# Attention and mixture of experts on one core: the second product's order of blocks, and the place of one copy on ScalarE

## The chip, the cores and the metric

The kernel runs on one core of a Trainium2 chip. The metric is the device time of one execution in microseconds (us). A core has five engines with a queue each: TensorE (PE, with PEld for its weight loads), VectorE (DVE), ScalarE (ACT), GpSimd (POOL) and SyncE (SP, which issues most of the DMAs). Each queue is worked off in its order, and an engine waits for another by a semaphore. TensorE multiplies into PSUM; ScalarE and VectorE read PSUM, GpSimd works in SBUF alone.

## The reference

```
attention, for each of 8 batches and 8 heads (S = 576, head size 64):
    scores = q k^T / 8 + cum[i] - cum[j]        # cum: cumulative sum of log(clip(f))
    out    = softmax(causal(scores)) v
x = all heads of a position side by side        # N = 4608 rows, D = 512
logits = x @ w_gate;  expert = argmax(logits);  gate = its softmax value
for e in range(8):                              # w1: 512 x 1024, w2: 1024 x 512
    xe = x[expert == e]
    out[expert == e] = gate * (relu(xe @ w1[e]) @ w2[e])
```

## The kernel before

Attention over all batches takes the first 340 us of the span, and expert 0 is worked in between and to 366 us. From there on experts 1 to 7 follow one another, each some 55 us long, and 6.6 us of closing work end the span. The change lies in experts 1 to 7 alone.

An expert has room for 640 rows. All matrices are kept as a rounded high part and the rest as a low part, so that one product takes three matmuls: high with high, high with low, low with high.

**First product** (`sevens`, `group`, `product`; its matmuls are L1421). x @ w1 is done with seven products of half-size blocks in the place of eight. The 1024 columns of h are eight blocks of 128, and group i (0 to 3) makes the blocks i and i + 4. A group has seven steps (s = 0 to 6) of six matmuls with 256 to 320 columns. They write four banks of PSUM, called a, b, g and d here: steps 0 to 3 start a, b, g, d, and steps 4 to 6 add to a, b, g. PE's order is steps 0 to 3 of group 0, then steps 4 to 6 of a group with steps 0 to 3 of the next in one branch, and last steps 4 to 6 of group 3.

What the other engines do is in `after(s)`, and is written into the queues in the order of the steps:

- s = 0: what is left of the group before (the list `self.ends`), and `p1 <- a` by ScalarE (L1475), the copy of the first product. Step 4 adds to a, so PE has to wait for this copy.
- s = 1: u2 = b + p1 by VectorE (L1479), which step 5 waits for; then `last` of the group before.
- s = 2: `p5 <- g` by ScalarE (L1482), which step 6 waits for. p1 and p5 are two buffers that all groups share.
- s = 4: ScalarE rectifies a into the high part of h (L1466), VectorE makes the low part, called the rest (L1469).
- s = 5: u3 = b + p1 (L1488) and d = u3 - d (L1489) by VectorE, p5 = u3 + p5 by GpSimd (L1490).
- s = 6: the rectifications left over go into `self.ends`: `end` (ScalarE rectifies d and p5; VectorE does g = g + u2, L1498, and the rest of d), then the rectification of g, then `last` (the rests of p5 and g). They run at s = 0 and 1 of the next group, and those of group 3 at the start of the second product.

The two halves of block i come from a and g, those of block i + 4 from d and p5. Between these steps ScalarE rounds weights (L1333, L1348), VectorE or GpSimd makes their low parts (L1339, L1349), GpSimd forms sums of the next expert's first weights (L1318 to L1321) and fetches its rows.

**Second product** (`down`; its matmuls are L1229). Five tiles of 128 rows; each runs over the eight blocks of h, three matmuls of 512 columns a block, into one bank, which ScalarE scales (L1237) and GpSimd scatters (L1238). In quarters of two blocks, work for the next expert is put in between: after the quarters 0, 2, 4, 6 and 8 PE turns 128 rows of it by four transposes (L1390) into one of the two banks of the pool `ps_t`, from which ScalarE and VectorE make the operands of its first product (`turn_t`, the last operation on the bank is the L1398 that writes xa).

The order on each engine is the order of the program's lines, with the lists `ups` (by step of the first product) and `dns` (by quarter of the second) setting what comes between.

Of the kernel before, what the change touches and what calls it, by code (L numbers as in the profile page):

```python
# [37 lines left out]
FT = FF // P  # L38
# [135 lines left out]
def psum(pool):  # L174
    return pool.tile([P, 512], F32, name="ps", tag="ps")
# [893 lines left out]
class Moe:  # L1069
# [149 lines left out]
    def down(self, e, m, part=(0, FT)):  # L1219

        c, nc = self.c, self.nc
        rows = self.rows_of_h(e, m)
        if part[0] == 0:
            self.py[m] = psum((c.ps_v, c.ps_m)[m % 2])
        py = self.py[m]
        for ft in range(*part):
            w = self.w2p[e, ft]
            for k, (hi_, wi) in enumerate(((0, 0), (0, 1), (1, 0))):
                c.note(nc.tensor.matmul(  # L1229
                    py, rows(hi_, ft), w[wi],  # L1230
                    start=(ft + k == 0), stop=(ft == FT - 1 and k == 2),
                ))
        if part[1] < FT:
            return
        _, si, g, s = self.index(e, m)
        y = c.yp.tile([P, D], F32, name="y")
        nc.scalar.activation(y, py, AF.Copy, scale=g[:, s : s + 1])  # L1237
        nc.gpsimd.indirect_dma_start(  # L1238
            out=self.out, out_offset=bass.IndirectOffsetOnAxis(ap=si[:, s : s + 1], axis=0),
            in_=y, in_offset=None, bounds_check=self.x_dram.shape[0] - 1, oob_is_err=False,  # L1240
        )
# [26 lines left out]
    def finish(self, run, t):  # L1268

        c = self.c  # L1270
        ends = []
        fx, lg = t["fx"], t["lg"]

        def indices():
            self.idx["all"] = table_indices(c, self.tc, c.rp, c.tab, NHI, "fast")
            arms(c, self.tc)
            self.begin_x(0, 1)
            for e, m in ((0, NA), (0, NA + 1), (1, 3), (1, 4)):
                self.fetch(e, m)

        up = lambda ft: lambda: self.up(0, 0, ft)
        down = lambda m, *part: lambda: self.down(0, m, part)
        turn = lambda m: lambda: ends.append(self.turn(0, m))
        end = lambda: ends.pop(0)()
        for f in (
            t["logits"], up(2), lambda: self.load_w2(0, 3),
            lg, t["softmax"], t["expert"], up(3), fx[0], t["gate"], up(4), t["rank"], fx[1],
            t["slot"], up(5), t["hi"], fx[2], t["lo"], up(6), fx[3], lambda: self.split_w2(0, 3),
            up(7), t["table"], fx[4], down(0, 0, 4), indices, down(0, 4, 8), down(1, 0, 4),
            down(1, 4, 8), down(2, 0, 4),  # L1290
            turn(NA), end, down(2, 4, 5), turn(NA + 1), end, down(2, 5, 8),
        ):
            run(f)
# [152 lines left out]
    def group(self, e, i):  # L1446

        c, nc = self.c, self.nc
        V, A, G = nc.vector, nc.scalar, nc.gpsimd
        pools = (c.ps_t, c.ps_t, c.ps_m, c.ps_v) if i % 2 == 0 else (c.ps_s,) * 3  # L1450
        a, b, g, d = [psum(p) for p in pools] + [c.ps_r] * (i % 2)
        a, b, g, d = (t[:, 0:HN] for t in (a, b, g, d))

        late = (e, i) == (1, 0)
        p1, p5 = (
            c.yp.tile([P, D], F32, name="y")[:, 0:HN] if late and k == 1 else c.values["u", k]
            for k in range(2)
        )
        us = {}
        hh, hl = self.h[e]  # L1460

        def place(h, f, n):
            return h[:, f * (FT // 2) + i].rearrange("p (s j) -> p j s", j=2)[:, n]

        def relu(src, *at):
            A.activation(place(hh, *at), src, AF.Relu)  # L1466

        def rest(src, *at):
            V.scalar_tensor_tensor(place(hl, *at), src, 0.0, place(hh, *at).bitcast(F32),  # L1469
                                   ALU.max, ALU.subtract)  # L1470

        def after(s):
            if s == 0:
                self.ends.pop(0)()
                A.copy(p1, a)  # L1475
                self.ends.pop(0)()
            elif s == 1:
                us[2] = self.up_.tile([P, HN], F32, name="u2")
                V.tensor_tensor(us[2], b, p1, ALU.add)  # L1479
                self.ends.pop(0)()  # L1480
            elif s == 2:
                A.copy(p5, g)  # L1482
            elif s == 4:
                relu(a, 0, 0)
                rest(a, 0, 0)
            elif s == 5:
                u3 = self.up_.tile([P, HN], F32, name="u3")
                V.tensor_tensor(u3, b, p1, ALU.add)  # L1488
                V.tensor_tensor(d, u3, d, ALU.subtract)  # L1489
                G.tensor_tensor(p5, u3, p5, ALU.add)  # L1490
            elif s == 6:
                self.ends = [end, lambda: relu(g, 0, 1), last]

        def end():
            relu(d, 1, 0)
            if not late:
                relu(p5, 1, 1)
            V.tensor_tensor(g, g, us[2], ALU.add)  # L1498
            rest(d, 1, 0)

        def last():
            if late:
                relu(p5, 1, 1)
            rest(p5, 1, 1)
            rest(g, 0, 1)

        steps = ((a, 0, 0, "B11", True), (b, 0, 1, "T2", True), (g, 0, 2, "T1", True),
                 (d, 0, 3, "T4", True), (a, 1, 0, "B21", False), (b, 1, 1, "T3", False),
                 (g, 1, 2, "B22", False))
        return steps, after  # L1510
# [333 lines left out]
```

## Time and profile before

| what | us |
|---|---|
| median of 3 runs | 757.97 (757.63 to 758.67) |
| profiled execution | 760.25 |
| its span, first to last instruction | 758.5 |
| PE busy | 739.9 (98%) |
| DVE, ACT, POOL busy | 542.4 (72%), 499.2 (66%), 514.8 (68%) |
| mean granted clock | 0.991 |
| expert 1, 366.2 to 424.5 | 58.3, PE busy 56.35, clock 0.97 |
| expert 2, 424.5 to 479.6 | 55.1, PE busy 54.68, clock 1.00 |
| expert 3, 479.6 to 534.2 | 54.6, PE busy 52.98 |
| expert 5, 589.3 to 643.7 | 54.4, PE busy 51.49 |

A matmul's record overlaps the next one's, since matmuls are pipelined: in a full stretch 512 columns are done every 0.23 us, though one record lasts 0.40. The distance between two starts tells the pace, and a pause shows as a longer distance.

### The profile page before, as it was taken

The page shows a single profiled execution, that of the slowest core. Times are in us where ns is not written, and L with a number is a line of the kernel's source. Part 1 is how long each engine was busy: PE and PEld are TensorE (multiplying, and loading weights), DVE is VectorE, ACT ScalarE, POOL GpSimd, SP SyncE. Part 2 cuts the span into 40 slices and gives each one's busy share as a digit, 9 for nine tenths or more (in the row PEclk, how much of TensorE's full clock was granted, in tenths as well). Part 3 has the DMA queues.
Part 4 walks back from the last instruction along what each step waited for, and adds up shares of the span by engine and source line. Part 5 has one row for each costly group of instructions (what it writes and reads, how often), then busy time and mean ns, then how long its engine had stood idle before and what let it go on. Part 6 is the DMA issues. An engine that isn't in the chain of part 4 may idle for free.

```text
span 758.5 us, 18648 instructions
## 1 busy us (share of the span) xinstructions
PE 739.9 (98%) x6464; PEld 632.8 (83%) x6464; DVE 542.4 (72%) x1596; ACT 499.2 (66%) x1319; POOL 514.8 (68%) x681
## 2 busy tenths in 40 slices
PE   8999999999999999999989999999999989999996
PEld 4888888888888888889988998978988978988975
DVE  6668898988898887625897488487586685784720
ACT  6999998989898987434665465455554653654621
POOL 6999998989898979644784574475465565565311
PEclk9999999999999999999999999999999999999998
DMA  6857778767766676243343523623622623523200
GB/s 199 215 150 206 198 206 198 211 197 199 209 201 208 194 204 182 96 136 103 123 161 111 176 76 112 195 71 97 202 83 89 209 81 104 168 85 106 73 29 34
DMA packets 78563, 111.85 MB, mean 147 GB/s; under 512 B 9327, under 2 KB 40047, under 8 KB 78448
## 3 DMA queue, kind: packets, MB, share of 16 engines
q1 hardware_dynamic: 71408, 90.38, 41.3%
q0 software_dynamic: 6400, 19.93, 8.0%
q8 instruction: 71, 1.16, 0.7%
q14 instruction: 44, 0.36, 0.1%
q10 hardware_dynamic: 640, 0.01, 0.0%
HBM read 91.26 MB, written 20.07 MB: 147 GB/s over the span
## 4 chain that ended last, share of the span: by engine, by line
PE 72%; DVE 15%; POOL 6%; ACT 3%; issue 2%; DMA 0%; POOLq 0%; DVEq 0%; ACTq 0%
PE ps L1229 27%; PE ps L525 11%; PE ps L402 9%; PE ps L454 7%; PE ps L1421 5%; DVE w_1w L1349 5%; PE ps L436 4%; DVE hl L1469 4%; POOL u L1490 3%; PE ps L449 2%; PE ps L1195 2%; ACT hhw L1466 2%; DVE w1s L1339 2%; POOL w L1086 1%; DVE u L1488 1%
## 5 line engine op out<-in xcount | busy, mean ns | idle before, releaser
L421 ACT ACTIVATE sc<-sc,nmx 128x512 f32<-128x512 f32 (+3 forms) x256 | 142.6, 560 | 5.2 <-DVE nmx L378 4.0
L1238 POOL DMA_INDIRECT out<-y,si_fast x40 | 42.0, 1050 | 119.4 <-ACT y L1237 74.9
L1229 PE MATMUL ps<-w_0w,hhw 128*128 128x512 f32 x280 | 114.2, 408 | 5.9 <-ACT hhw L1466 5.9
L1229 PE MATMUL ps<-w_0w,hl 128*128 128x512 f32 x280 | 111.3, 398 | 0.0
L1229 PE MATMUL ps<-w_1w,hhw 128*128 128x512 f32 x280 | 111.1, 397 | 0.0
L1421 PE MATMUL ps<-X_0w,w1s 128*128 128x320 f32 (+2 forms) x504 | 107.4, 303 | 0.2 <-ACT u L1482 0.2
L466 ACT COPY aT<-ps 128x512 f32<-128x512 f32 (+1 forms) x224 | 93.3, 506 | 1.9 <-PE ps L454 1.2
L329 POOL TENSOR_TENSOR hl<-raw,hl 128x640 fp32r<-128x640 f32 (+1 forms) x60 | 89.6, 1493 | 5.0
L525 PE MATMUL ps<-aT,va_t 128*64 128x256 f32 (+3 forms) x896 | 90.3, 353 | 0.0
L1421 PEld LDWEIGHTS ps<-X_0w,w1s 128*128 128x128 f32 x504 | 82.2, 188 | 0.8 <-ACT u L1482 0.4
L1237 ACT ACTIVATE y<-ps,g_fast 128x512 f32<-128x512 f32 x40 | 27.6, 691 | 81.8 <-PE ps L1229 76.2
L402 PE MATMUL ps<-hl 64*128 64x512 f32 (+1 forms) x720 | 80.1, 340 | 0.0
L525 PEld LDWEIGHTS ps<-aT,va_t 128*64 128x64 f32 x896 | 56.1, 137 | 28.5 <-issue 5.0
L1421 PE MATMUL ps<-X_1w,w1s 128*128 128x320 f32 (+2 forms) x252 | 75.8, 301 | 0.0
L1229 PEld LDWEIGHTS ps<-w_0w,hhw 128*128 128x128 f32 x280 | 52.8, 188 | 19.2 <-ACT hhw L1466 9.0
L378 DVE CUSTOM_DVE_ANT_0 sc<-ps,bias 128x128 f32<-128x128 f32 (+1 forms) x128 | 59.8, 486 | 9.2 <-PE ps L402 2.4
L1229 PEld LDWEIGHTS ps<-w_0w,hl 128*128 128x128 f32 x280 | 53.0, 189 | 14.4 <-DVE hl L1469 2.1
L1490 POOL TENSOR_TENSOR u<-u,u 128x320 f32<-128x320 f32 x27 | 23.8, 881 | 59.0 <-DVE u L1488 55.5
L1229 PEld LDWEIGHTS ps<-w_1w,hhw 128*128 128x128 f32 x280 | 53.0, 189 | 10.2
L378 DVE CUSTOM_DVE_ANT_1 sc<-ps,bias 128x256 f32<-128x256 f32 (+1 forms) x128 | 57.7, 487 | 2.8 <-PE ps L402 2.8
L1421 PE MATMUL ps<-xa,w1s 128*128 128x320 f32 (+2 forms) x336 | 56.2, 302 | 3.0 <-ACT u L1475 3.0
L1339 DVE TENSOR_TENSOR w1s<-w1r,w1s 128x1024 fp32r<-128x1024 f32 (+1 forms) x42 | 49.1, 1183 | 11.9 <-ACT w1s L1333 10.2
(247 smaller groups left out, 1894.0 us busy)
## 6 DMA issues: line engine op xcount, KB each, us to landing
bias<-ud SPq DMA_DIRECT2D x30, 576.0 KB, 7.0
w1r<-in_w SPq DMA_DIRECT2D x112, 128.0 KB, 2.9
w<-in_w SPq DMA_DIRECT2D x28, 512.0 KB, 4.2
raw<-in_qkT SPq DMA_DIRECT2D x64, 160.0 KB, 3.2
raw<-in_qkT SPq DMA_DIRECT2D x64, 144.0 KB, 3.7
va_t<-in_va SPq DMA_DIRECT2D x32, 256.0 KB, 5.8
x_dram<-row SPq DMA_DIRECT2D x32, 256.0 KB, 2.8
wraw<-in_w SPq DMA_DIRECT2D x7, 512.0 KB
```

The costliest lines, as they stand in the source:

```text
L329: return eng.tensor_tensor(hl[:, 1], raws[n][:, r : r + w], hl[:, 0].bitcast(F32), ALU.subtract)
L378: red_last[:] = [V.tensor_tensor_reduce(dst, src, in1, -0.125, init, ALU.add, ALU.min, nms[n][:, col : col + 1]).ins]
L402: note(nc.tensor.matmul(pb[j][:, o : o + w], q[js], k[js], start=(i == 0), stop=(i == len(terms) - 1),))
L421: A.activation(x, x, AF.Exp, bias=nms[n][:, 5 * j + t : 5 * j + t + 1], scale=-1.0, accum_out=ssums[b][:, t, 2 * p + j : 2 * p + j + 1])
L454: note(nc.tensor.transpose(out.bitcast(F32R), words, c.identr[rows, rows]))
L466: copy_on = {"a": lambda o, i: A.copy(o, i), "v": lambda o, i: V.tensor_copy(o, i)}
L525: note(nc.tensor.matmul(pv[j * HD : (j + 1) * HD, q0 - qa : qb - qa], l, r, start=(blk == 0), stop=(blk == nb - 1),))
L1229: c.note(nc.tensor.matmul(py, rows(hi_, ft), w[wi], start=(ft + k == 0), stop=(ft == FT - 1 and k == 2),))
L1238: nc.gpsimd.indirect_dma_start(out=self.out, out_offset=bass.IndirectOffsetOnAxis(ap=si[:, s : s + 1], axis=0), in_=y, in_offset=None, bou ...
L1339: (eng or self.nc.vector).tensor_tensor(lo, raw, hi.bitcast(F32), ALU.subtract)
L1421: self.nc.tensor.matmul(bank[:, 0:cols], w[:, wi, mat, kt], x[xi][:, kt, 0:cols], start=start and k == 0, stop=k == 5, skip_group_check=True,)
L1490: G.tensor_tensor(p5, u3, p5, ALU.add)
```

## The change

In experts 1 to 7 each tile of the second product takes the blocks in the order 0, 1, 2, 4, 5, 6, 3, 7, so that the two blocks of group 3 come last; expert 0 keeps its order. And at s = 0 ScalarE copies p1 ahead of `end` of the group before, where it stood between `end` and the rectification of g.

```
         if part[0] == 0:
             self.py[m] = psum((c.ps_v, c.ps_m)[m % 2])
         py = self.py[m]
-        for ft in range(*part):
+        for n in range(*part):
+            ft = (0, 1, 2, 4, 5, 6, 3, 7)[n] if e else n
             w = self.w2p[e, ft]
             for k, (hi_, wi) in enumerate(((0, 0), (0, 1), (1, 0))):
                 c.note(nc.tensor.matmul(
                     py, rows(hi_, ft), w[wi],
-                    start=(ft + k == 0), stop=(ft == FT - 1 and k == 2),
+                    start=(n + k == 0), stop=(n == FT - 1 and k == 2),
                 ))
...
         def after(s):
             if s == 0:
+                A.copy(p1, a)
                 self.ends.pop(0)()
-                A.copy(p1, a)
                 self.ends.pop(0)()
```

All lines below the first piece stand one line further down in the changed kernel, up to the copy.

PE in the first tile of an expert's second product, after its first two blocks; w_0 are the weights of blocks 0 to 3, w_1 those of 4 to 7, hhw and hl the high and the low part of h. Before:

```order
L1390 MATMUL ps<-identr,xg 128x128 [waits DMASW1_49,PE_49]
L1390 MATMUL ps<-identr,xg 128x128 x3
L1229 MATMUL ps<-w_0_0w,hhw 128x512
L1229 MATMUL ps<-w_0_1w,hhw 128x512
L1229 MATMUL ps<-w_0_0w,hl 128x512 [waits DVE_49]
L1229 MATMUL ps<-w_0_0w,hhw 128x512 [waits Activation_49]
L1229 MATMUL ps<-w_0_1w,hhw 128x512
L1229 MATMUL ps<-w_0_0w,hl 128x512 [waits DVE_49]
L1229 MATMUL ps<-w_1_0w,hhw 128x512
```

Now:

```order
L1391 MATMUL ps<-identr,xg 128x128 [waits DMASW1_49,PE_49]
L1391 MATMUL ps<-identr,xg 128x128 x3
L1230 MATMUL ps<-w_0_0w,hhw 128x512
L1230 MATMUL ps<-w_0_1w,hhw 128x512
L1230 MATMUL ps<-w_0_0w,hl 128x512 [waits DVE_49]
L1230 MATMUL ps<-w_1_0w,hhw 128x512
...
L1391 MATMUL ps<-identr,xg 128x128 [waits DMASW2_49,PE_49]
L1391 MATMUL ps<-identr,xg 128x128 x3
L1230 MATMUL ps<-w_0_0w,hhw 128x512 [waits Activation_49]
L1230 MATMUL ps<-w_0_1w,hhw 128x512
L1230 MATMUL ps<-w_0_0w,hl 128x512 [waits DVE_49]
```

Block 3, whose first matmul waits for ScalarE and its third for VectorE, moved from behind block 2 to behind the second set of transposes.

ScalarE at the last change of group in an expert's first product, from the rectification of a; pr is d, u_104 is p5, u_96 is p1, ps the banks a and g. Before:

```order
L1466 ACTIVATE hhw<-ps 128x320 [waits PE_49]
L1466 ACTIVATE hhw<-ps 128x320 [waits DVE_49]
L1466 ACTIVATE hhw<-u_104 128x320 [waits Pool_49]
L1475 COPY u_96<-ps 128x320 [waits PE_49]
L1466 ACTIVATE hhw<-ps 128x320 [waits DVE_49]
L1348 CAST w_1_0w<-w_1_1_102 128x1024 [waits DMAHW6_49]
L1482 COPY u_104<-ps 128x320 [waits DVE_49,PE_49,Activation_49]
```

Now:

```order
L1467 ACTIVATE hhw<-ps 128x320 [waits PE_49]
L1475 COPY u_96<-ps 128x320 [waits DVE_49,PE_49]
L1467 ACTIVATE hhw<-ps 128x320 [waits DVE_49]
L1467 ACTIVATE hhw<-u_104 128x320 [waits Pool_49]
L1467 ACTIVATE hhw<-ps 128x320 [waits DVE_49]
L1349 CAST w_1_0w<-w_1_1_102 128x1024 [waits DMAHW6_49]
L1483 COPY u_104<-ps 128x320 [waits DVE_49,PE_49]
```

The copy of p1 moved ahead of the rectifications of d and p5, and waits for VectorE now, which reads p1 last in u3 of the group before. The order on VectorE and GpSimd is the same as before.

## Rows read from the trace of the kernel before

**Rows 1.** Waits of the whole span: waiter, what it waited for, total us, times, longest
```profile
PE ps L1229 <- ACT hhw L1466: 5.9, 7, 1.7
PE ps L1421 <- ACT u L1475: 3.0, 5, 1.0
```

**Rows 2.** Timeline, PE, expert 3: start, length, line, operation, [idle before <-releaser]
```profile
503.22 0.40 PE L1229 MATMUL ps<-w_0w,hhw 128*128 128x512 f32 x1
...
505.45 0.40 PE L1229 MATMUL ps<-w_0w,hl 128*128 128x512 f32 x1
506.88 0.50 PE L1229 MATMUL ps<-w_0w,hhw 128*128 128x512 f32 x1 [1.03 <-ACT hhw L1466]
...
507.82 0.39 PE L1229 MATMUL ps<-w_0w,hhw 128*128 128x512 f32 x1
```

**Rows 3.** Timeline, PE, first tile of expert 1's second product
```profile
393.72 0.40 PE L1229 MATMUL ps<-w_0w,hl 128*128 128x512 f32 x1
395.83 0.64 PE L1229 MATMUL ps<-w_0w,hhw 128*128 128x512 f32 x1 [1.72 <-ACT hhw L1466]
...
399.58 0.46 PE L1390 MATMUL ps<-identr,xg 128*128 128x128 f32 x4
```

**Rows 4.** Windows: stretch, length, busy PE, PEld, DVE, ACT, POOL, clock, DMA, GB/s
```profile
397.00:398.20 1.20, 1.20 (x4) 0.91 (x4) 0.96 (x4) 1.20 (x3) 1.04 (x3) 0.50 0.00 0
```

**Rows 5.** Timeline, PE, block 3 of expert 7's first tile
```profile
725.49 0.50 PE L1229 MATMUL ps<-w_0w,hhw 128*128 128x512 f32 x1 [0.47 <-ACT hhw L1466]
```

**Rows 6.** Timeline, ScalarE and VectorE, expert 3: the last rectifications and rests
```profile
506.01 0.49 ACT L1466 ACTIVATE hhw<-u 128x320 fp32r<-128x320 f32 x1 [0.83 <-POOL u L1490]
506.40 0.43 ACT L1466 ACTIVATE hhw<-ps 128x320 fp32r<-128x320 f32 x1
...
506.94 0.48 DVE L1469 SCALAR_TENSOR_TENSOR hl<-ps,hhw 128x320 fp32r<-128x320 f32 x1
```

**Rows 7.** Timeline, PE, expert 3: last matmul of step 3, step 4, step 6
```profile
499.82 0.29 PE L1421 MATMUL pr<-X_1w,w1s 128*128 128x288 f32 x1
500.70 1.06 PE L1421 MATMUL ps<-xa,w1s 128*128 128x288 f32 x6 [0.59 <-ACT u L1475]
...
502.40 0.44 PE L1421 MATMUL ps<-X_0w,w1s 128*128 128x288 f32 x2
```

**Rows 8.** Timeline, VectorE, then ScalarE, same change of group
```profile
498.28 0.48 DVE L1488 TENSOR_TENSOR u<-ps,u 128x320 f32<-128x320 f32 x1
...
500.68 0.49 DVE L1479 TENSOR_TENSOR u<-ps,u 128x320 f32<-128x320 f32 x1 [0.37 <-ACT u L1475]
...
499.32 0.46 ACT L1466 ACTIVATE hhw<-ps 128x320 fp32r<-128x320 f32 x1 [2.26 <-DVE ps L1489]
...
500.25 0.40 ACT L1475 COPY u<-ps 128x320 f32<-128x320 f32 x1
...
501.83 0.44 ACT L1482 COPY u<-ps 128x320 f32<-128x320 f32 x1
```

**Rows 9.** Timeline, GpSimd and VectorE, same place: sum of weights, rest of p5
```profile
500.58 0.74 POOL L1319 TENSOR_TENSOR w1r<-w1r 128x256 f32<-128x256 f32 x1
501.09 0.58 DVE L1469 SCALAR_TENSOR_TENSOR hl<-u,hhw 128x320 fp32r<-128x320 f32 x1
```

**Rows 10.** Timeline: fifth transposes (PE), last readers of turns 1 and 3 (DVE), experts 3, 1
```profile
518.67 0.46 PE L1390 MATMUL ps<-identr,xg 128*128 128x128 f32 x4
...
508.99 0.42 DVE L1398 TENSOR_TENSOR xa<-ps,xa 128x256 fp32r<-128x256 f32 x1
...
516.56 0.42 DVE L1398 TENSOR_TENSOR xa<-ps,xa 128x256 fp32r<-128x256 f32 x1
...
409.04 0.46 PE L1390 MATMUL ps<-identr,xg 128*128 128x128 f32 x4
...
397.93 0.42 DVE L1398 TENSOR_TENSOR xa<-ps,xa 128x256 fp32r<-128x256 f32 x1
...
405.98 0.42 DVE L1398 TENSOR_TENSOR xa<-ps,xa 128x256 fp32r<-128x256 f32 x1
```

More of the change, by code (lines that the diff above doesn't have):

```diff
@@ L1225, in down @@
         py = self.py[m]
-        for ft in range(*part):
+        for n in range(*part):
+            ft = (0, 1, 2, 4, 5, 6, 3, 7)[n] if e else n
             w = self.w2p[e, ft]
@@ L1230, in down @@
                     py, rows(hi_, ft), w[wi],
-                    start=(ft + k == 0), stop=(ft == FT - 1 and k == 2),
+                    start=(n + k == 0), stop=(n == FT - 1 and k == 2),
                 ))
@@ L1473, in after @@
             if s == 0:
+                A.copy(p1, a)
                 self.ends.pop(0)()
-                A.copy(p1, a)
                 self.ends.pop(0)()
```

## The prediction

> **What bounds the kernel now.** I read in this order: the mean granted clock (0.991, and nearly all of the span at full clock), the share of busy time (PE 98%), the waits of PE, then PE's rows in order of time at each wait, then ScalarE, VectorE and GpSimd at the same places. PE is the bound nearly everywhere, so its stalls are lost time, and only two kinds fall in experts 1 to 7: seven waits of the second product for a rectification (L1466), and five of the first product for the copy of L1475 [rows 1]. The view counts only what is left after the modelled end of the matmul before, 5.9 and 3.0 us. The loss is larger, from start to start.
>
> In expert 3 the second product starts at 503.22. Its first nine matmuls and one set of transposes take 2.46 us (505.45 and one step of 0.23 more). Block 3 should follow at 505.68, starts at 506.88, and its last part waits for VectorE; block 4 starts at 507.82 instead of 506.38 [rows 2]. The loss is **1.44 us**. Done in the same way, experts 2, 4, 5, 6 and 7 lose 0.84, 0.84, 1.55, 1.12 and 0.89 us (the last of the seven is shown [rows 5]). In expert 1 the gap of 2.1 us is followed by nine matmuls at 0.43 us a step [rows 3], at a granted clock of 0.50, that is 1.2 GHz [rows 4]. From 393.72 to the transposes at 399.58 there are 5.86 us for ten steps, which are 2.30 at full clock: a loss of **3.56 us**, of which about 1.65 is the slow clock. All seven: **10.24 us**.
>
> What ends this wait last is a chain outside PE: GpSimd's sum (L1490) lets ScalarE rectify p5 at 506.01, behind it g at 506.40 (block 3's second half, done at 506.83), and VectorE's rest of g is done at 507.42 [rows 6].
>
> **The change, part by part.** *Order of the blocks.* No instruction is added. Block 3 becomes the seventh of eight. Two runs of nine matmuls and a transpose set stand ahead of it then, 4.9 us after the product's start (in expert 7, which turns no rows, 18 steps or 4.2). In expert 3 that is 508.1; the rectification is done at 506.83, the rest 0.6 later and is read two steps after the first matmul [rows 2, 6]. Slack 1.3 us: the stall goes. Expert 1 is the tightest: its chain ends 4.3 us after the start, and I find the slack to be about nothing there, which costs at most some 0.3 us. With no gap of two microseconds, I expect the slow clock to go too. Blocks 4 to 6 are read earlier by one place; they and their weights were written microseconds before. In the last tile block 3 is read 2.1 us later, so the loads of the next expert's second weights, which overwrite it, wait longer; they are first rounded nine steps of the first product later (some 8 us), and a load of this size lands in 4.2 us. This costs nothing.
>
> *The copy ahead of the rectifications.* In expert 3's last change of group VectorE finishes u3 (L1488) at 498.76, the last thing that the copy's destination waits for, and ScalarE waits for VectorE's L1489 until 499.32. The copy of 0.40 us fits into that idle time, from 498.80, instead of at 500.25 [rows 8]. So the step-4 wait goes (0.75 us from 499.82 to 500.70, less one step of 0.13, and 0.1 for the slow restart after it [rows 7]). But the wait does not vanish, it moves. Step 6 needs the copy of p5 (L1482), which was done at 502.27 [rows 8]; PE without the first wait would want it at 501.54, 0.86 before the 502.40 at which step 6 started [rows 7]. ScalarE could do that copy 0.3 us earlier, since everything behind L1475 moves up by its 0.30. It also overwrites what VectorE's rest of p5 still reads, and that ends at 501.67.
>
> Will this rest come earlier, now that VectorE's L1479 no longer waits 0.37 for the copy [rows 8]? The trace says no: it took 0.58, against 0.48 of the same operation with an input in PSUM [rows 6], and ended 0.35 after GpSimd's L1319, which ended at 501.32 [rows 9]. GpSimd's place hangs on L1490, which the change doesn't move. The Trainium skill, "SBUF — State Buffer", section "SBUF: two separate sides", states it as a lock: a VectorE operation with two SBUF inputs and a GpSimd operation that reads SBUF exclude one another for a whole instruction. By that rule, the trace agrees, the 0.37 us is swallowed; without it the chain would run 0.3 us ahead, and the sum below would be 0.9 us larger.
>
> So the copy of p5 runs at 501.71 to 502.15 and step 6 at 502.19: a gain of 0.21 us, not 0.85. In the same way I get 0.36, 0.12 and 0.40 us for experts 1, 5 and 7; experts 2, 4 and 6 have no such wait. Bounds of this part: the whole of it, about 4.4 us start to start, if nothing took its place; and a loss, because at an expert's first change of group PE is not ahead: there the rectifications now stand behind a copy that waits for PE's step 0, and come some 0.3 us later. The same lock swallows that too; if not, the chain is 0.3 us late and three experts lose 0.3 each. I take the nearer end, the rows above.
>
> *What is late next.* The chain of ScalarE, VectorE and GpSimd does not get faster, PE does. After the stall the five transposes of the second product share two banks of PSUM, and the fifth needs the third's, which VectorE frees with the last operation of that turn. In expert 3 it ends at 516.98 and the fifth transposes stood at 518.67 [rows 10]. PE may gain 518.67 − 517.02 = **1.65 us** there, just what the two terms (1.44 + 0.21) ask for. Expert 5 has the same 1.65. In expert 1 the third turn would be freed at 406.44, and 0.48 earlier where it no longer waits for PE (from the first turn to the third it takes 8.05 us there and 7.57 in expert 3): 405.96, against 409.04, so of 3.56 + 0.36 only **3.08 us** can be had [rows 10]. Experts 2, 4, 6 have 0.5 to 0.8 us to spare.
>
> *Sum:* 3.08 + 0.84 + 1.65 + 0.84 + 1.65 + 1.12 + (0.89 + 0.40) = **10.5 us**. The profiled execution took 760.25 us, 1.75 more than its span; it would take 749.8. The runs' median is 757.97, 2.3 below the profiled one; taking the same from it gives **747.5 us**.
>
> **The rivals.** *The chain does not hold PE back.* Then all stalls and the copy's gains stand: 10.24 + 1.09 = 11.3 us, 746.6; and if p5's copy did not hold PE either, 743.4. For: a bank's last reader is inferred from the code and the order. Against: the rows of the chain show hardly any slack in expert 1.
>
> *The chain comes later.* Each us costs one us in experts 1, 3 and 5, whose transposes then wait. Half a microsecond gives 749.0; the slow clock staying in expert 1 costs 0.8 more, 749.8. For: the late rectifications at an expert's first change. Against: in these places VectorE waits for GpSimd anyway [rows 9].
>
> *Slower than before.* The mechanism is the copy heading ScalarE's queue: where PE's step 0 of the next group is late, both rectifications and VectorE's rests wait behind it. A chain late by d loses 7d − 3.0 of the 10.5 us (all seven experts past their slack), so it decides at d = 1.9 us in an expert; at 2.3 the time is 760.6. Three changes of group would have to lose over 0.6 each. Against: only the first finds PE behind, by 0.3; at the last, VectorE's u3 (498.76) comes well after PE has done step 0 of the next group, since PE only waits two steps of work later [rows 7].
>
> That the change does not do what it says is no rival: the order of instructions shows both moves in all seven experts.
>
> **How the numbers follow.** About 0.2% (1.5 us) can be told from no change. Forecast, 747.5 with its own range of 746.5 to 748.7: 0.6. The chain not binding, 743.4 to 746.6: 0.15. The chain later or the clock still low, 748.7 to 752: 0.22. Slower: 0.03. The range takes the forecast, most of the second and most of the third, 744.8 to 750.8. Faster 0.95, same 0.03, slower 0.02 (part of the slower rival ends within 0.2%).
>
> **What would show it.** Right: no wait of PE's L1229 for L1466 left, or one of under 0.4 us in expert 1; full granted clock after expert 1's second product starts; waits for L1475 replaced by shorter ones for L1482 in experts 1, 3, 5 and 7; short waits of the transposes for VectorE's L1398 in expert 1. Wrong: block 3 still waits by over 0.5 us, waits for L1482 that are as long as those for L1475 were, the transposes of experts 2, 4 or 6 waiting, or new waits of the first product for weights or for turned rows.

## The result, and the profile after

Three comparisons, each beside the kernel before:

| changed kernel, median us | before, median us | difference | ratio, 95% interval |
|---|---|---|---|
| 750.67 (4 runs) | 758.32 (4 runs) | 7.65 | 0.9895 [0.9877, 0.9912] |
| 749.19 (4 runs) | 759.44 (17 runs) | 10.25 | 0.9861 [0.9844, 0.9879] |
| 749.99 (5 runs) | 758.40 (9 runs) | 8.41 | 0.9890 [0.9873, 0.9908] |

The 13 runs of the changed kernel have a median of 749.99 us, the 30 of the kernel before in these comparisons one of 758.82: 8.83 us less. The forecast of 747.5 us was 2.5 too low. The time lies inside the stated range of 744.8 to 750.8, by the first comparison (750.67) only just, and the sign was right.

The waits of PE after (columns as in [rows 1]; lines behind the first piece of the diff are one higher now):

```profile
PE ps L1422 <- ACT u L1483: 1.9, 4, 0.8
...
PE ps L1422 <- DVE u L1480: 0.3, 1, 0.3
PE ps L1391 <- ACT X_0w L1401: 0.2, 1, 0.2
PE ps L1391 <- issue: 0.2, 1, 0.2
```

Both rows of [rows 1] are gone: the second product (now L1230) has no wait for a rectification left, and none of the first product is for the copy of p1. New are four waits for the copy of p5 (L1483), one of 0.3 us for VectorE's u2 (L1480), and two small ones of transposes (L1391), one after the other in expert 1.

Windows after: expert 1, expert 3, and the stretch of expert 1 in which the gap of [rows 3] stood (columns as in [rows 4]):

```profile
366.80:421.98 55.18, 54.78 (x310) 48.60 (x309) 43.26 (x79) 30.52 (x61) 38.77 (x39) 1.00 0.41 133
476.30:529.70 53.40, 52.98 (x310) 46.80 (x309) 38.58 (x76) 29.49 (x60) 31.79 (x32) 1.00 0.40 129
391.60:396.80 5.20, 5.20 (x29) 4.27 (x28) 4.98 (x10) 1.93 (x6) 4.87 (x5) 1.00 0.19 52
```

Expert 1 went from 58.1 to 55.2 us, expert 3 from 54.5 to 53.4. PE is busy through the third window, at full clock, where 2.1 us lay between two starts before.

PE after in expert 1: the second product's start, the second transposes and block 3 behind them (its first matmul and its third, which reads the rest), the last two transposes; then what block 3 needs from ScalarE and VectorE, and VectorE's last reads of the banks of turns 2 and 3:

```profile
391.67 0.39 PE L1230 MATMUL ps<-w_0w,hhw 128*128 128x512 f32 x1
...
396.21 0.45 PE L1391 MATMUL ps<-identr,xg 128*128 128x128 f32 x4
396.50 0.47 PE L1230 MATMUL ps<-w_0w,hhw 128*128 128x512 f32 x1
...
397.03 0.39 PE L1230 MATMUL ps<-w_0w,hl 128*128 128x512 f32 x1
...
402.85 0.51 PE L1391 MATMUL ps<-identr,xg 128*128 128x128 f32 x4 [0.18 <-issue]
...
406.44 0.51 PE L1391 MATMUL ps<-identr,xg 128*128 128x128 f32 x4 [0.20 <-ACT X_0w L1401]
```

```profile
395.75 0.44 ACT L1467 ACTIVATE hhw<-ps 128x320 fp32r<-128x320 f32 x1
...
396.30 0.48 DVE L1470 SCALAR_TENSOR_TENSOR hl<-ps,hhw 128x320 fp32r<-128x320 f32 x1
...
402.33 0.42 DVE L1399 TENSOR_TENSOR xa<-ps,xa 128x256 fp32r<-128x256 f32 x1
...
405.92 0.42 DVE L1399 TENSOR_TENSOR xa<-ps,xa 128x256 fp32r<-128x256 f32 x1
```

Block 3 starts 4.83 us after the product does. The last rectification was done at 396.19, so it had 0.3 us to spare, and the last rest (done at 396.78) is read at 397.03. What is late next are the last two transposes: the steps between the five are 3.17, 3.15, **3.49** and **3.59** us, where 3.15 is the undisturbed one. The profile names ScalarE's L1401 for one of these two waits and nothing for the other. But VectorE's L1399, the last reader of the bank that each of them needs, ends at 402.75 and 406.34, 0.10 us ahead of the transposes both times; the forecast had named it (L1398 before).

The last change of group in expert 3 after, on PE, ScalarE, VectorE, GpSimd:

```profile
498.28 0.29 PE L1422 MATMUL ps<-X_1w,w1s 128*128 128x288 f32 x1
499.00 0.53 PE L1422 MATMUL ps<-X_0w,w1s 128*128 128x288 f32 x2 [0.42 <-ACT u L1483]
...
495.60 0.43 ACT L1475 COPY u<-ps 128x320 f32<-128x320 f32 x1 [1.79 <-DVE u L1489]
...
497.32 1.04 ACT L1349 CAST w_0w<-w 128x1024 fp32r<-128x1024 f32 x1
498.52 0.43 ACT L1483 COPY u<-ps 128x320 f32<-128x320 f32 x1 [0.17 <-DVE hl L1470]
...
497.37 1.06 DVE L1470 SCALAR_TENSOR_TENSOR hl<-u,hhw 128x320 fp32r<-128x320 f32 x1
...
497.34 0.74 POOL L1320 TENSOR_TENSOR w1r<-w1r 128x256 f32<-128x256 f32 x1
```

The copy of p1 stands in ScalarE's idle time, as forecast. The copy of p5 waits for VectorE's rest of p5, which ends at 498.43, and that is 0.35 us after GpSimd's sum, as in [rows 9]. Measured from the start of expert 3's first product (476.32 here, 479.63 before), the copy of p5 starts at 22.20 us in both kernels.

Expert 7 turns nothing for a next expert, and GpSimd forms no sums there. VectorE and ScalarE after, the same place in expert 7:

```profile
712.20 0.48 DVE L1470 SCALAR_TENSOR_TENSOR hl<-u,hhw 128x320 fp32r<-128x320 f32 x1
...
712.14 1.04 ACT L1349 CAST w_0w<-w 128x1024 fp32r<-128x1024 f32 x1
713.07 0.43 ACT L1483 COPY u<-ps 128x320 f32<-128x320 f32 x1
```

The same rest takes 0.48 us in place of 1.06, and the copy of p5 is held by ScalarE's rounding instead.

### The profile page after: what moved, and what is told of

Its sections match the earlier page's. It is cut to its first block, busy times and chain, and to the rows that moved or that the text cites. A ratio compares the mean times of both kernels' runs of the same rounds, so it can differ in the third digit from the quotient of the medians.

```text
span 749.4 us, 18668 instructions
## 1 busy us (share of the span) xinstructions
PE 736.5 (98%) x6464; PEld 631.6 (84%) x6464; DVE 543.5 (73%) x1596; ACT 498.2 (66%) x1319; POOL 515.4 (69%) x681
## 3 DMA queue, kind: packets, MB, share of 16 engines
q8 instruction: 71, 1.16, 0.6%
## 4 chain that ended last, share of the span: by engine, by line
PE 90%; DVE 4%; POOL 3%; issue 1%; ACT 1%; DMA 0%; ACTq 0%; POOLq 0%; DVEq 0%
PE ps L1230 29%; PE ps L1422 17%; PE ps L525 11%; PE ps L402 10%; PE ps L454 7%; PE ps L436 4%; PE ps L1195 3%; PE ps L449 3%; PE ps L1391 1%; PE ps L616 1%; PE pr L1422 1%; DVE w_1w L1350 1%; POOL w L1086 1%; DVE hl L1470 1%; PE pr L1017 1%
## 5 line engine op out<-in xcount | busy, mean ns | idle before, releaser
L1230 PE MATMUL ps<-w_0w,hhw 128*128 128x512 f32 x280 | 113.1, 404 | 0.0
L1230 PE MATMUL ps<-w_1w,hhw 128*128 128x512 f32 x280 | 110.5, 395 | 0.0
L1230 PE MATMUL ps<-w_0w,hl 128*128 128x512 f32 x280 | 110.1, 393 | 0.0
L1230 PEld LDWEIGHTS ps<-w_0w,hl 128*128 128x128 f32 x280 | 52.7, 188 | 12.8
L1230 PEld LDWEIGHTS ps<-w_0w,hhw 128*128 128x128 f32 x280 | 52.5, 187 | 10.9
L1230 PEld LDWEIGHTS ps<-w_1w,hhw 128*128 128x128 f32 x280 | 52.7, 188 | 10.3
L1334 ACT CAST w1s<-w1r 128x1024 fp32r<-128x1024 f32 (+1 forms) x56 | 52.1, 943 | 9.1 <-POOL w1r L1320 9.1
```

The lines of the kernel that those rows point to most:

```text
L1230: c.note(nc.tensor.matmul(py, rows(hi_, ft), w[wi], start=(n + k == 0), stop=(n == FT - 1 and k == 2),))
L1334: self.nc.scalar.copy(t[:, 0], raw)
```

## Experiments

Stretches in this and the next section run from the first matmul of an expert's first product to that of the next expert (in expert 7 to the last matmul of its second product), and are split at the start of the second product.

### The new order alone, the copy in its old place

```
-                A.copy(p1, a)
                 self.ends.pop(0)()
+                A.copy(p1, a)
                 self.ends.pop(0)()
```

> The order of the blocks alone; the copy of p1 stays where it was before the change. Mine: the seven waits of the second product go (8.1 to 8.5 us by the stretches of the two traces in hand), the five waits of step 4 for L1475 stay as in the kernel before (first-product stretches of 25.1, 23.6, 23.1 and 23.6 us in experts 1, 3, 5, 7), expert 1's transposes wait 0.2 us less. Sum against the kernel before some 8.4 to 9 us in the trace, so the copy is worth under 1 us. Rival: the copy's move carries about 3 us of the gain, then this run gains only some 5 to 6 us.

Measured: 749.74 us beside 759.44, ratio 0.9868 [0.9850, 0.9885]; the changed kernel in the same comparison 0.9861 [0.9844, 0.9879]. The waits of PE for the copy are those of [rows 1] again:

```profile
PE ps L1422 <- ACT u L1476: 3.0, 5, 1.0
```

The order of the blocks carries all of the gain that runs can tell. The stretches of experts 1 to 6 are 55.17, 54.32, 53.35, 54.34, 52.84, 54.28 us, against 55.19, 54.34, 53.36, 54.29, 52.83, 54.35 in the first profile of the changed kernel. The copy did gain 0.21 us in expert 1's first product (25.09 to 24.88), and the second product gave back 0.23 (30.08 to 30.31): the step from the third to the fourth transposes is 3.26 us here and 3.49 in the changed kernel.

### The copy alone, the old order

> The copy ahead of the rectifications alone; blocks in their old order. Mine: the first-product stretches get shorter by 0.6 us in sum over the experts 1, 3, 5 and 7, but the chain that releases block 3 does not move, so the seven waits of the second product get longer by as much: no difference, within 0.5 us. Rival (the copy frees PE): 3.0 to 4.4 us faster. Second rival (the rectifications come later at each change of group): 1 to 2 us slower.

Measured: 760.18 us (12 runs) beside 759.44, ratio 1.0005 [0.9993, 1.0018]: no change. Its first products are those of the changed kernel (24.86 in expert 1, 23.56 in expert 3), and the waits of its PE:

```profile
PE ps L1229 <- ACT hhw L1466: 7.0, 7, 1.9
PE ps L1421 <- ACT u L1482: 1.9, 4, 0.8
```

The stall of the second product grew from 5.9 to 7.0, which takes back what the first products gained. ScalarE in expert 2 of this kernel, whose first product starts at 424.18; the same instruction in the second profile of the kernel before (start at 423.44); and in the changed kernel (start at 421.98):

```profile
451.20 0.49 ACT L1466 ACTIVATE hhw<-u 128x320 fp32r<-128x320 f32 x1 [0.82 <-POOL u L1490]
...
450.19 0.49 ACT L1466 ACTIVATE hhw<-u 128x320 fp32r<-128x320 f32 x1 [0.84 <-POOL u L1490]
...
449.02 0.50 ACT L1467 ACTIVATE hhw<-u 128x320 fp32r<-128x320 f32 x1 [0.82 <-POOL u L1491]
```

That is 27.02 us after the start with the copy alone, 26.75 before, and 27.04 in the changed kernel. So the rectifications behind the copy do make the chain some 0.3 us later in expert 2, as much in expert 4, and 0.2 in expert 6; in experts 1, 3, 5 and 7 it is not later by more than 0.1. In the changed kernel block 3 does not notice: in expert 2 it starts 29.44 us after the first product does, in place of 27.62.

### Both kernels again

> The changed kernel once more. Mine: its experts 1 to 7 take the same stretches as in the trace in hand (55.2, 54.3, 53.4, 54.3, 52.8, 54.4, 51.1 us) to 0.3 us each, so that what differs between executions lies before 366 us; 7 to 9 us faster than the kernel before. Rival: the stretches of the experts themselves differ by a microsecond or more between executions.

> The kernel before once more, for a second trace. The profiled execution was 2.3 us above its median. Theory A: TensorE's clock fell in expert 1 there and does not fall in every execution; then this trace shows expert 1 in 56.5 us with full granted clock after the gap. Theory B: the clock falls there every time (expert 1 takes 58.1 us again) and the 2.3 us lie before 366 us, in attention.

> The changed kernel itself, a third time, beside the kernel before. Theory by the profiles (8.4 us by stretches without the slow clock in expert 1, up to 1.1 more in executions where it comes): a gain of 8.4 to 9.6 us on average over many runs of both, so a ratio of 0.987 to 0.989. Rival by the first two pairings alone: 7.65 or 10.25 us, 0.990 or 0.9865.

> The kernel before itself, for one more profile. Theory: the pause of 2.1 us in expert 1's second product is there in every execution, and the fall of the clock to half behind it only in some, so that the product takes either 31.9 us or 33.0 us there; the six other stalls repeat within 0.1 us. Rival (the slow clock follows every such pause, and the one profile without it was the exception): 33.0 again.

> The kernel before itself, for one more profile, with the same two theories as for the third one: 31.9 or 33.0 us for expert 1's second product if the clock falls only sometimes, 33.0 if it falls after every such pause.

Nothing is edited in these five. The changed kernel's runs stand in the table on top. In the second comparison its experts kept their stretches to 0.3 us, as expected, but the gain of 10.25 us was outside the 7 to 9 expected; the third gave 8.41 us, at the lower end of the 8.4 to 9.6 that the profiles gave. The single executions of the kernel before took 759.54, 756.76 and 759.93 us. In the first of these expert 1 took 56.97 us, with the full clock behind the gap. That is 1.15 less than in the profile of the forecast, but the whole time was only 0.7 shorter (759.54 against 760.25).

PE in the second profile of the kernel before, block 3 of expert 1's first tile, and the window of 2.3 us from there:

```profile
395.90 0.50 PE L1229 MATMUL ps<-w_0w,hhw 128*128 128x512 f32 x1 [1.74 <-ACT hhw L1466]
```

```profile
395.90:398.20 2.30, 2.30 (x9) 1.67 (x10) 1.82 (x8) 1.58 (x5) 2.15 (x4) 1.00 0.01 2
```

The same place in the fourth profile:

```profile
397.15 0.50 PE L1229 MATMUL ps<-w_0w,hhw 128*128 128x512 f32 x1 [1.73 <-ACT hhw L1466]
```

```profile
397.10:399.40 2.30, 2.25 (x9) 1.68 (x10) 1.82 (x8) 1.58 (x5) 2.19 (x3) 1.00 0.02 7
```

The clock (the third value from a window's end) is 1.00 in both, and in the third profile too, against 0.50 in the profile that the prediction was made from [rows 4]. The gap is the same every time and the fall of the clock to half is not: it came in one profile of four. The kernel with the copy alone has a longer gap (2.34 us from start to start) and kept the full clock as well. Without the fall the second product of expert 1 took 31.8 to 31.9 us, with it 33.0.

### Other banks for the last three turns

```
-        pt = psum(c.ps_t)
+        pt = psum(c.ps_s if e > 1 and m < NA else c.ps_t)
```

> The changed kernel, with the last three turns of the next expert's rows in each second product written to three other banks of PSUM, which stand idle there, and no longer to the two banks of the first two turns. Theory (in expert 1 the fourth and fifth transposes wait for a bank that the second and third turn still read): these two waits go, the steps between the five transposes in expert 1 are all 3.14 to 3.18 us (before this edit 3.46 to 3.49 and 3.58 to 3.59 for the last two), and expert 1's second product takes 29.6 to 29.9 us in place of 30.3 to 30.55; the other experts stay within 0.1 of 29.7 to 29.85. Rival (the transposes wait for rows that arrive late, or for ScalarE): expert 1 stays at 30.3 or more.

The five transposes of expert 1 in this kernel:

```profile
393.00 0.45 PE L1391 MATMUL ps<-identr,xg 128*128 128x128 f32 x4
...
396.12 0.46 PE L1391 MATMUL ps<-identr,xg 128*128 128x128 f32 x4
...
399.28 0.46 PE L1391 MATMUL ps<-identr,xg 128*128 128x128 f32 x4
...
402.42 0.46 PE L1391 MATMUL ps<-identr,xg 128*128 128x128 f32 x4
...
405.56 0.46 PE L1391 MATMUL ps<-identr,xg 128*128 128x128 f32 x4
```

Steps of 3.12 to 3.16 us, no wait, and 29.69 us for expert 1's second product in place of 30.31 to 30.55; the others stayed at 29.75. The two shared banks did hold expert 1, for 0.6 to 0.9 us, and only expert 1 to a tenth. (The 30.31 is from the one profile in which the stretch behind the fifth transposes ran at the faster of two paces, see the last section. At equal pace, 30.55 against 29.69, it is 0.86.) One execution took 750.34 us; half a microsecond is not told by that.

### What holds the copy of p5

Three kernels, each the changed one with a part more. First, a rounding of second weights moved out of ScalarE's way:

```
-                for i, k in enumerate((15, 22, 16, 23) if e == 1 else (9, 15, 16, 22)):
+                for i, k in enumerate((15, 23, 16, 26) if e == 1 else (9, 15, 16, 26)):
```

> The changed kernel, with ScalarE's rounding of a block of second weights (1.04 us, L1349) moved from ahead of the copy of p5 at the last change of group to behind d of the same group. Theory (the copy of p5 is held by VectorE's rest of p5, which lies beside GpSimd's sum of weights): the first products of experts 1, 3 and 5 get less than 0.15 us shorter (from 24.89, 23.59, 22.99), the copy still waits for VectorE's rest; in expert 7, where GpSimd forms no sums, the copy stands right behind the rounding, so there the wait of 0.15 goes and the first product takes about 23.1 in place of 23.32. Rival (ScalarE's own queue holds the copy everywhere): 0.5 us or more less in each of experts 1, 3 and 5.

VectorE, ScalarE and GpSimd in expert 3 of this kernel:

```profile
498.25 1.05 DVE L1470 SCALAR_TENSOR_TENSOR hl<-u,hhw 128x320 fp32r<-128x320 f32 x1
...
499.39 0.42 ACT L1483 COPY u<-ps 128x320 f32<-128x320 f32 x1 [1.09 <-DVE hl L1470]
...
498.21 0.74 POOL L1320 TENSOR_TENSOR w1r<-w1r 128x256 f32<-128x256 f32 x1
```

ScalarE now stands idle for 1.09 us ahead of the copy, and the first products of experts 1, 3, 5 are as long as before (24.86, 23.59, 22.99); expert 7's fell from 23.32 to 23.02. Both as the theory had it. The rest ends at 499.30, again 0.35 us after GpSimd's sum.

Second, with that, GpSimd's first four sums moved from behind group 2 to behind group 3:

```
-                       (20, N(self.sums_s, 0)), (20, fetch(e + 1, 0)),
-                       (27, N(self.sums_s, 1)))
+                       (20, fetch(e + 1, 0)),
+                       (27, N(self.sums_s, 0)), (27, N(self.sums_s, 1)))
```

> As the kernel with the rounding moved, with one buffer for p5, and with GpSimd's first four sums of the next expert's weights moved from behind p5 of group 2 to behind p5 of group 3, so that GpSimd does nothing beside VectorE's rest of p5. Theory (VectorE's rest of p5, two operands in SBUF, does not end while GpSimd's sum runs): the rest's record shrinks from 1.06 to about 0.48 us in experts 1, 3 and 5, the copy of p5 follows it, and the first products get 0.4 to 0.6 us shorter than with the rounding moved alone. Rival (the rest is held by ScalarE's rectification of p5 or by its own reads): the record stays at 1.06 and the first products at their length. Later work may pay for the late sums; that is not judged here.

VectorE and ScalarE in expert 3:

```profile
496.79 0.48 DVE L1470 SCALAR_TENSOR_TENSOR hl<-u,hhw 128x320 fp32r<-128x320 f32 x1
...
497.37 0.43 ACT L1483 COPY u<-ps 128x320 f32<-128x320 f32 x1 [0.52 <-DVE hl L1470]
```

Without GpSimd beside it the same rest takes 0.48 us. First products: 24.59, 23.03, 22.43 us in experts 1, 3, 5, that is 0.27, 0.56 and 0.56 less. Expert 1 gained less than the 0.4 forecast: 24.6 is also what experts 2, 4 and 6 take in every profile, which show none of these waits, so this seems to be what the matmuls alone take.

Third, the rounding moved and a second buffer for p5 in every second group (`p5 = self.up_.tile([P, HN], F32, name="p5b")` where `i % 2`), the sums in their place:

> As the kernel with the rounding moved, and with a second buffer for p5 in every second group, so that the copy of p5 no longer overwrites what VectorE's rest of p5 reads. Theory (rest of p5 is what holds the copy, by this buffer alone): no wait for the copy of p5 is left, and the first products of experts 1, 3, 5, 7 take about 24.2, 23.0, 22.4, 23.1 us (0.7, 0.6, 0.6 and 0.25 less than in the changed kernel). Rival (PE's own step 2, or the last reader of the bank, holds it): as in the kernel with the rounding moved alone.

First products 24.59, 22.79, 22.10, 22.78 us in experts 1, 3, 5, 7: a larger gain than forecast in three of them, a smaller one in expert 1. Of the waits for the copy of p5 one of 0.2 us is left, in expert 5. The rest of p5 held the copy, by the buffer that they share, and GpSimd held the rest. All three kernels lose in second products, above all in expert 1: 31.7 us with the rounding moved, with one buffer or two, and 32.1 with the sums late, against 30.3 to 30.55. By the waits, the transposes stand longer there, and the second product waits for a rest again (1.0 us in the first kernel, 0.5 in the others). The moved rounding, which all three share, is enough for this, as the first kernel shows; by which step it does so is not shown. The single executions took 755.79, 752.65 and 750.13 us.

### The parts that held, together

The banks, the second p5, and the rounding moved in experts 3, 5 and 7 alone.

> The changed kernel with three of the edits tried together: the last three turns in three other banks of PSUM, a second buffer for p5 in every second group, and the rounding of second weights moved behind d in experts 3, 5 and 7 alone. If the parts hold as measured singly: second products of experts 1 to 6 all 29.7 to 29.9 us, first products of experts 3, 5, 7 at 22.8, 22.1, 22.8 us, expert 1's 24.7 to 24.9; against the changed kernel 0.7 in expert 1, 0.8, 0.9 and 0.5 in experts 3, 5 and 7, together about 2.9 us, a ratio to the changed kernel of about 0.996. Rival (the moved rounding delays the chain of the second product in those experts also with the banks apart): the second products of experts 3, 5 come out 0.3 us or more longer, and the ratio is over 0.9975.

Measured: 747.13 us (5 runs), ratio to the kernel before 0.9854 [0.9834, 0.9875]; the changed kernel beside it took 749.99, so 0.9962 of that, as forecast; the slowest run here (748.14) is below the fastest there (748.78). Windows of experts 1 and 3:

```profile
367.40:421.77 54.37, 54.37 (x309) 48.64 (x308) 43.12 (x79) 30.31 (x61) 38.61 (x39) 1.00 0.40 131
476.11:528.66 52.55, 52.55 (x310) 46.70 (x308) 38.25 (x76) 29.18 (x60) 31.06 (x32) 1.00 0.41 131
```

PE is busy through all of both, and by the waits only 0.6 us are left in experts 1 to 7, all in expert 5 (0.4 for u2, 0.2 for the copy of p5). First products 24.60, 22.79, 22.09, 22.79 us in experts 1, 3, 5, 7, second products 29.75 to 29.78 in experts 1 to 6.

## Why the prediction was right, and where it was off

The gain by expert, in us. "Before" is the mean of the three profiles without the slow clock, "changed" that of its three profiles; the last column is the first profile of each, the one of before that the prediction was made from:

| expert | forecast | before | changed | gain | gain against the first profile |
|---|---|---|---|---|---|
| 1 | 3.08 | 56.96 | 55.36 | 1.60 | 2.93 |
| 2 | 0.84 | 55.12 | 54.36 | 0.76 | 0.77 |
| 3 | 1.65 | 54.73 | 53.27 | 1.46 | 1.16 |
| 4 | 0.84 | 55.15 | 54.31 | 0.84 | 0.85 |
| 5 | 1.65 | 54.41 | 52.83 | 1.58 | 1.59 |
| 6 | 1.12 | 55.46 | 54.35 | 1.11 | 1.11 |
| 7 | 1.29 | 51.89 | 51.08 | 0.81 | 1.15 |
| sum | 10.47 | | | 8.16 | 9.56 |

With both sides at the slower of two paces of PE (last section) experts 1, 3 and 7 gain 1.5, 1.4 and 1.1 us, and the sum is 8.3.

**Right: the seven stalls and their chain.** All seven are gone, and experts 2, 4, 5 and 6 gained their term within 0.1. At equal pace expert 3 gained its 1.44 for the order to a tenth, and expert 7's second product its 0.89 (28.65 to 27.76). The order alone gives all of the gain that runs can tell.

**Right: what is late next.** In expert 1 the banks of the turns give back 0.84 by the forecast, 0.6 to 0.9 by the kernel with other banks. The fifth transposes stand 39.65 us after expert 1's start; the forecast (405.96, less the start at 366.40) was 39.56. The fourth wait as well, not only the fifth.

**Right in kind, too large: the copy.** The wait went from the copy of p1 to that of p5, as forecast, for the reason given: GpSimd's sum holds VectorE's rest, in the changed kernel, and the two kernels made for it show both sides. The Trainium skill, "SBUF — State Buffer", section "SBUF: two separate sides", has this as a lock; the rest's 0.48 us without the sum, and 1.05 with it, agree. But the four gains of 0.36, 0.21, 0.12 and 0.40 us were 0.2, 0.0, 0.1 and 0.25 in the first products. The mis-sized step is that the copy of p5 would run at 501.71 in expert 3, 0.04 behind the rest and some 0.1 ahead of where it ran. It starts 0.09 behind the rest now, and the rest ends 22.11 us after the start of the first product in place of 22.04: GpSimd's place did not move forward, so the copy's did not either. In expert 7, where no sums stand beside it, the rounding on ScalarE is the limit.

**Wrong: "the same lock swallows that too".** The rectifications behind the copy did make the chain 0.2 to 0.3 us later in experts 2, 4 and 6, as the kernel with the copy alone shows. It cost nothing because the new order has that slack, not because of GpSimd.

**Wrong: the slow clock as a steady loss.** The term of 3.56 us for expert 1 holds 1.4 to 1.65 of slow clock (the step from the first to the second transposes was 6.69 us with it and 5.30 without). The three later profiles have no such fall. The forecast may even have counted it twice: it took 2.3 us off to come from the profiled execution to the median, and the profiled one was above the median of 30 runs (758.82) by 1.43, about what that fall of the clock cost. That the fall put it there is not shown: the fourth profile's execution kept the full clock at this place and took 759.93, 1.11 above the same median. An event that is in the profile and not in the median can be taken off in one of the two places, not in both. The Trainium skill, "TensorE: Matmul & The Clock Gate", section "Part 1: The HAM clock gate (the "warmup" mystery)", says of the half clock at a kernel's start that the same kernel has a different number of matmuls at it from run to run. The four profiles show such a difference for a fall behind a gap: one in four has it.

So 747.5 becomes 749.99 in two steps. The median of three runs that it started from was 0.85 us below that of thirty (757.97 and 758.82). The gain is 8.83 by these medians, not 10.5, of which experts 1 to 7 without the slow clock have 8.2 to 8.3. The remaining 0.5 to 0.7 is not settled: an execution in four with the slow clock would make 0.3 of it by estimate, and the start of expert 1 alone varies between 364.2 and 368.3 us over the profiles, which the change cannot reach.

**The rivals.** That the chain does not bind: excluded for the banks in expert 1 and for the copy of p5. That the chain comes later: true by up to 0.3 us, within the slack everywhere. By its time alone the result lies in this rival's band (748.7 to 752) and not in the forecast's own (746.5 to 748.7), but neither of the rival's causes is there: no wait for a rectification is left, and the clock in expert 1 is full in the three profiles. Slower: no sign of it.

## What to carry to other kernels

When a consumer loops over blocks that a chain on other engines finishes, and their sum does not depend on the order, read last what is finished last: it costs no instruction, and it hides later delays of that chain too. Before moving one operation of a shared queue ahead, look at what holds the next one that the waiting engine needs; here it was an engine (GpSimd) that neither the copy nor its reader names. And of an event of the clock look at a second profile before it becomes a term, and never take it off both as a term and by way of the median.

## What the hardware showed that was not expected

**VectorE beside GpSimd.** The rest of p5, with both inputs in SBUF, ended 0.35 us after GpSimd's sum in four places: in expert 3 of the kernel before (501.67 and 501.32), of the changed kernel (498.43 and 498.08) and of that with the rounding moved (499.30 and 498.95), and in expert 1 of the changed kernel (390.12 and 389.77). Its record was 1.05 to 1.07 us where it was due soon after the sum's start, and 0.58 in the kernel before, where it was due late; without a sum it is 0.48. What the sum costs it depends on when it comes, its end does not. In experts 1 to 6 of the changed kernel all twelve rests of p5 that met such a sum ended 0.35 to 0.37 us after it.

**Two paces at full clock.** Matmuls of 512 columns at a granted clock of 1.00 follow one another every 0.233 us or every 0.229 us. Expert 7's second product, 119 steps without a wait, took 27.76 us in all three profiles of the changed kernel and 27.25 in that with the order alone and in the combined one. In the kernel before, what follows the fifth transposes took 15.48 us in experts 1 and 3 of the first profile, and 15.75 in the other three. Expert 7's second product in the first profile of the changed kernel, and in the kernel with the order alone (120 matmuls; a window also counts records that reach in from its neighbours):

```profile
714.47:742.23 27.76, 27.76 (x122) 22.37 (x120) 3.05 (x7) 4.08 (x7) 4.81 (x5) 1.00 0.10 39
...
716.11:743.36 27.25, 27.25 (x121) 22.36 (x120) 3.06 (x7) 4.05 (x7) 4.80 (x5) 1.00 0.10 39
```

The pace is why expert 3 seemed to gain only 1.16 us and expert 7 anything from 0.8 to 1.15. What sets the pace stays open. A difference of 0.3 to 0.5 us in such a product is put down to an edit only where both ran at the same pace.

**The clock behind a gap.** A gap of PE of 2.1 us was followed by the half clock for some 3 us in one profile of four, and by the full clock in the other three and after one of 2.34 us.
